# Half-precision parts in place of fp32r parts in the feed-forward of a fused attention and max-out kernel

## The chip, the cores and the metric

The kernel runs on one core of a Trainium2 chip. The metric is the device time of one execution in microseconds. The engines are named as the profile names them: PE (TensorE, matrix products; PEld is its weight loads), DVE (VectorE), ACT (ScalarE), POOL (GpSimd) and SP (SyncE, which here only issues DMAs).

## The reference

Two stages follow each other. The first is a linear attention with a decaying state, token by token, for 4 sequences, 8 heads, 768 tokens and 48 channels per head. The second takes its output as 3072 tokens of 384 features through three 384 x 768 products, an element-wise maximum, and a 768 x 384 product.

```python
for t in range(S):
    kt, vt, rt = (k[:, :, t], v[:, :, t], r[:, :, t])
    cur = np.einsum('bhd,bhe->bhde', u[None] * kt, vt)
    y[:, :, t] = np.einsum('bhd,bhde->bhe', rt, state + cur)
    state = w[None, :, :, None] * state + np.einsum('bhd,bhe->bhde', kt, vt)
...
h = np.maximum(np.maximum(x @ w1, x @ w2), x @ w3)
return (h @ w_out).astype(np.float32)
```

The inputs of the attention are float32; the four weight matrices are float64. k, r and v are normal with a spread of 0.1, the decay w lies between 0.85 and 0.95, and the weights have a spread of one over the square root of their row count.

## The kernel before, in words

**Work.** The 768 tokens of each sequence are cut into 12 chunks of 64, so that a chunk is 256 tokens of the 4 sequences. For each chunk there are two halves q (4 heads each). Per half the attention makes scores (L412, r against k within the chunk, masked), values (L449, scores against v plus r against the state) and keys (L432, k against v, added to the state at L438). All of this is done in pairs of half-precision parts: each float32 operand is a high part and a low part, and `three` (L408) adds high x high, high x low and low x high, 64 or 48 columns each. The left operands kb, ktb, vb and sb are block matrices that `spread` (L319) makes by two DMAs from the dense kd, ktd, vd and sd. In chunk 0 the products are plain float32 instead (`full`, L479).

**Feed-forward.** The values of both halves become the feature-major x of a chunk in two parts, xh (ACT, L464) and xl (DVE, L468), both fp32r. For each of 6 blocks f of the hidden size and each of the 3 matrices, `up` (L490) adds 9 products of 128 x 128 weights against 256 tokens: xh and xl against the high weights, xh against the low weights. ACT copies the first of three results out of PSUM (L499), DVE takes the maximum with the second and the third (L503). The hidden value m is split into hh (ACT, L506) and hl (POOL or DVE, L512), and `down` (L524) makes three output tiles of 18 products each. A chunk thus has 162 products up and 54 down, 216 of 256 columns, and the kernel 2592. An fp32r product is one instruction that loads its own weights.

**Weights.** The float64 weights come in 16 half tiles of 590 KB. For each, ACT and DVE in turn do `tops` (L240), `convert` (L243), `round_up` (L247, high part) and `leave` (L250, low part); all of this falls into chunks 0 and 1. They are loaded a second time near the end for a test of their lowest bits (L262, L266).

**Guards.** Sums of squares of r, k, v and the state (L348, on ACT) and some other numbers are compared with limits at the end (`check`, L554); a one-column product counts the partitions that pass (L565), DVE makes a flag (L569), and every engine reads it into a register (L911). If a partition fails, a general, slow part (L576) computes everything again.

**Order.** The order of all instructions is fixed before the kernel is built. Each step is given to `Plan.do` with an engine, a due time in chunks, a cost and the buffers it takes; `Plan.order` lays them out engine by engine, and the table `SHIFT` moves the due time of each kind of step. Every engine then works strictly through its own list. For chunks 0 to 2 the scaling of k and r, the product r u k and the decay (L367, L386, L387, L406) stand on DVE; from chunk 3 on they stand on POOL (L361).

Of the kernel before, what the change touches and what calls it, by code (L numbers as in the profile page):

```python
# [8 lines left out]
F32R = mybir.dt.float32r  # L9
# [25 lines left out]
SC_X = 2.0 ** -23  # L35


class Plan:
# [21 lines left out]
    }  # L60

    def __init__(self, bufs):
        self.bufs, self.todo, self.wrote, self.read = bufs, [], {}, {}

    def do(self, due, eng, cost, fn, reads=(), writes=(), takes=(), size=0, near=0):
# [6 lines left out]
        late = due > self.OPENING  # L72
        due += self.SHIFT.get(kind, (0, 0))[late]
# [8 lines left out]
        self.todo.append(dict(n=n, due=due, eng=eng, cost=cost, fn=fn, need=need, takes=takes, size=size, near=near, kind=kind, late=late, touch={*reads, *writes, *new}))  # L82
# [68 lines left out]
def kernel(ctx, tc, feat, tok, wu, ut, ws, wo, cst, out):  # L151
    nc = tc.nc
    const = ctx.enter_context(tc.tile_pool(name="const", bufs=1))
    raw = ctx.enter_context(tc.tile_pool(name="raw", bufs=3))
# [5 lines left out]
    hp = ctx.enter_context(tc.tile_pool(name="hp", bufs=1))  # L160
    wld = ctx.enter_context(tc.tile_pool(name="wld", bufs=4))
# [85 lines left out]
    def round_up(n, h, raw):  # L247
        nc.scalar.copy(out=part_of(n, h)[0], in_=mids(raw).bitcast(F32))
# [37 lines left out]
    tkf = hp.tile([P, NP, 2, C], F32, name="hl")  # L286
# [58 lines left out]
    stat = const.tile([P, 4, 2 * NCH], F32, name="stat")  # L345
    nc.vector.memset(stat[:, 3], 0.0)

    def square_sum(src, kind, c, q, scale=1.0):  # L348
        junk = tmp.tile([P, U, D], BF16, name="junk", bufs=1)
        nc.scalar.activation(out=junk, in_=src, func=AF.Square, scale=scale, accum_out=stat[:, kind, 2 * c + q:2 * c + q + 1])  # L350
# [117 lines left out]
    def x_low(c, q, xh, xl):  # L468
        ps = raws[c, q].pop("va")
        for (hi, src), (lo, _) in zip(x_parts(xh, q, ps), x_parts(xl, q, ps)):  # L470
            nc.vector.scalar_tensor_tensor(out=lo, in0=src, scalar=SC_X, in1=hi.bitcast(F32), op0=ALU.mult, op1=ALU.subtract)  # L471
# [18 lines left out]
    def up(x, f, i, n):  # L490
        ps = psm.tile([P, n], F32, name="psm")
        prods = [(wup[:, f, i, j, :], t[:, j, :]) for j in range(NJ) for t in x]
        prods += [(by_up(lows[f], i, j), x[0][:, j, :]) for j in range(NJ)]
        pairs3(ps, prods)
        return ps

    def first(ps, n):
        m = tmp.tile([P, n], F32, name="m", bufs=3)
        nc.scalar.copy(out=m, in_=ps)  # L499
# [11 lines left out]
    def h_low(c, h, f, m):  # L511
        lows_by(c, f).tensor_tensor(out=h[1][:, f, :], in0=m, in1=h[0][:, f, :].bitcast(F32), op=ALU.subtract)  # L512

    def up_all(x, h, f, n):
        for i in range(3):
            ps = up(x, f, i, n)
            if i == 0:
                m = first(ps, n)
            else:
                least(ps, m, m)  # L520
        h_high(h, f, m)
        h_low(0, h, f, m)

    def down(h, m, fs, banks, n):  # L524
# [4 lines left out]
        prods = [(t, hh[:, f, :]) for f in fs for t in (wdn[:, f, ms], by_down(lows[NF + f // 3], f, ms))]  # L529
        prods += [(wdn[:, f, ms], hl[:, f, :]) for f in fs]  # L530
        pairs3(banks[m], prods, 0 in fs, NF - 1 in fs)

    def leaving(ps, n):
        o = tmp.tile([P, n], F32, name="io", bufs=3)
        nc.scalar.copy(out=o, in_=ps)  # L535
# [40 lines left out]
    def general():  # L576
        def convert_any(n, h):
            hi, lo = part_of(n, h)
            rw = load_weight(n, h).bitcast(I32)[:, 0:2 * HN].rearrange("p (n two) -> p n two", two=2)
            t = raw.tile([P, HN], I32, name="tok")  # L580
            e = raw.tile([P, HN], I32, name="tok")
            m = hp.tile([P, HN], I32, name="hh")
# [13 lines left out]
            t = t.bitcast(F32)  # L596
            nc.scalar.copy(out=hi, in_=t)
# [378 lines left out]
```

## Time and profile before

| what | value |
|---|---|
| median of 3 runs (lowest to highest) | 414.68 us (414.3 to 416.64) |
| span of the profiled execution | 413.4 us |
| PE busy, of the span | 393.2 us, 95% |
| DVE busy | 283.6 us, 69% |
| ACT busy | 256.1 us, 62% |
| POOL busy | 183.2 us, 44% |
| DMA, mean | 218 GB/s, 90.08 MB |

The span runs from the first to the last instruction. It is 1.28 us under the median of the runs; that difference stands here for what lies around the span. Busy time of PE is that of matmuls whose ends overlap, so the rate of PE is read from the starts of successive matmuls in the timeline and not from the mean duration of one. The first feed-forward product starts at 28.97 us; what is ahead of it is loading, the float32 attention of chunk 0 and the first weights.

### The profile page before, as it was taken

To read this page: it belongs to the slowest core of one execution; us is meant where nothing else is said; L and a number is where in the kernel's file an instruction comes from. 1 tells how busy PE (TensorE), PEld (TensorE's weight loads), DVE (VectorE), ACT (ScalarE), POOL (GpSimd) and SP (SyncE) were. 2 spreads that over 40 slices of the span, in tenths; PEclk is the share of its full clock that TensorE was granted. 3 is DMA by queue.
4 is the path that set the end of the run, shared out by engine and by line. 5 is a ranking of instruction groups with operands and counts; after the bars stand their busy time and mean duration, and the time that the engine had idled before them with its cause. 6 is when DMAs were issued, how large, how long until landed. Compare 5 with 4: busy or idle time off the path is not lost.

```text
span 413.4 us, 11975 instructions
## 1 busy us (share of the span) xinstructions
PE 393.2 (95%) x4758; PEld 388.5 (94%) x4758; DVE 283.6 (69%) x550; ACT 256.1 (62%) x674; POOL 183.2 (44%) x180
## 2 busy tenths in 40 slices
PE   2869999999999999999999999999999999999996
PEld 2759999999999999999999999999999999999995
DVE  6888999988688766767667666567676596354240
ACT  5999987885766556456456456466456477265231
POOL 9000000298668754674664654754574551020120
PEclk9999999999999999999999999999999999999999
DMA  7899998889799997786785786785885996886101
GB/s 286 320 314 212 255 307 285 223 224 293 207 276 239 248 226 186 224 225 158 226 223 139 247 214 162 233 222 148 239 222 142 310 301 148 243 304 203 38 2 41
DMA packets 30954, 90.08 MB, mean 218 GB/s; under 512 B 4784, under 2 KB 9648, under 8 KB 30896
## 3 DMA queue, kind: packets, MB, share of 16 engines
q1 hardware_dynamic: 25568, 84.47, 72.1%
q10 hardware_dynamic: 5328, 4.82, 3.7%
q8 instruction: 38, 0.62, 0.7%
q14 instruction: 20, 0.16, 0.2%
HBM read 45.85 MB, written 4.72 MB: 122 GB/s over the span
## 4 chain that ended last, share of the span: by engine, by line
PE 65%; DVE 3%; ACT 3%; DMA 2%; issue 1%; POOL 1%; ACTq 0%; SPq 0%; DVEq 0%
PE psm L488 55%; PE psa L410 10%; DMA sb<-sd 2%; ACT junk L350 1%; DVE kd L338 1%; DVE state L446 0%; ACTq L874 0%; DVE m L503 0%; ACT io L535 0%; ACT xh L466 0%; DVE am L420 0%; POOL feat L367 0%; DVE hl L512 0%; ACT kd L333 0%; DVE sd L340 0%
## 5 line engine op out<-in xcount | busy, mean ns | idle before, releaser
L488 PE MATMUL psm<-xh,wh 128*128 128x256 f32 x648 | 166.6, 287 | 4.9 <-ACT xh L466 2.9
L488 PE MATMUL psm<-xl,wh 128*128 128x256 f32 x648 | 163.6, 282 | 1.1 <-DVE xl L471 1.1
L488 PEld LDWEIGHTS psm<-xh,wh 128*128 128x128 f32 x648 | 123.4, 190 | 5.7 <-ACT xh L466 3.1
L488 PEld LDWEIGHTS psm<-xl,wh 128*128 128x128 f32 x648 | 123.0, 190 | 1.4 <-DVE xl L471 1.4
L488 PE MATMUL psm<-xh,wl 128*128 128x256 f32 x648 | 112.9, 284 | 0.0
L503 DVE TENSOR_TENSOR m<-psm,m 128x256 f32<-128x256 f32 x144 | 60.4, 420 | 63.2 <-PE psm L488 54.5
L488 PEld LDWEIGHTS psm<-xh,wl 128*128 128x128 f32 x648 | 93.1, 190 | 0.0
L367 POOL TENSOR_TENSOR feat<-feat,wrt 128x512 f32<-128x512 f32 x36 | 47.1, 1319 | 74.7 <-DVE sd L340 68.9
L512 POOL TENSOR_TENSOR hl<-m,hh 128x256 fp32r<-128x256 f32 x55 | 46.5, 847 | 73.8 <-ACT hh L506 73.7
L506 ACT CAST hh<-m 128x256 fp32r<-128x256 f32 x72 | 28.8, 404 | 57.0 <-DVE m L503 56.7
L488 PE MATMUL psm<-hh,woh 128*128 128x256 f32 x216 | 54.3, 284 | 0.0
L488 PE MATMUL psm<-hh,wl 128*128 128x256 f32 x216 | 53.4, 279 | 0.0
L386 POOL TENSOR_TENSOR am<-tok,u_sb 128x384 f32<-128x384 f32 x18 | 21.0, 1165 | 58.0 <-DVE al L430 58.0
L350 ACT ACTIVATE junk<-tok 128x384 bf16<-128x384 f32 x72 | 37.5, 520 | 14.6 <-DMA tok<-in_tok_dram 12.0
L488 PEld LDWEIGHTS psm<-hh,woh 128*128 128x128 f32 x216 | 40.6, 188 | 0.0
L488 PEld LDWEIGHTS psm<-hh,wl 128*128 128x128 f32 x216 | 40.6, 188 | 0.0
L471 DVE SCALAR_TENSOR_TENSOR xl<-psa,xh 32x256 fp32r<-32x256 f32 (+2 forms) x60 | 28.3, 471 | 14.5 <-ACT xh L466 13.6
L466 ACT ACTIVATE xh<-psa 32x256 fp32r<-32x256 f32 (+2 forms) x60 | 25.0, 417 | 16.4 <-PE psa L410 15.4
L488 PE MATMUL psm<-hl,woh 128*128 128x256 f32 x216 | 35.1, 280 | 0.0
L338 DVE TENSOR_TENSOR kd<-feat,kd 128x512 f16<-128x512 f32 x22 | 20.5, 933 | 19.6 <-ACT kd L333 19.6
L410 PE MATMUL psa<-ah,vb 128*128 128x64 f16 x352 | 32.9, 194 | 0.0
L410 PE MATMUL psa<-rh,sb 128*128 128x64 f16 x352 | 32.5, 193 | 0.0
(98 smaller groups left out, 742.0 us busy)
## 6 DMA issues: line engine op xcount, KB each, us to landing
tok<-in_tok_dram SPq DMA_DIRECT2D x24, 576.0 KB, 6.8
raw<-in_ws_dram SPq DMA_DIRECT2D x24, 576.0 KB, 7.4
feat<-in_feat_dram SPq DMA_DIRECT2D x24, 512.0 KB, 5.4
kb<-kd SPq DMA_DIRECT2D x22, 256.0 KB, 5.9
kb<-kd SPq DMA_DIRECT2D x22, 248.0 KB, 6.1
ktb<-ktd SPq DMA_DIRECT2D x20, 256.0 KB, 3.4
ktb<-ktd SPq DMA_DIRECT2D x20, 248.0 KB, 4.5
raw<-in_wo_dram SPq DMA_DIRECT2D x8, 576.0 KB, 5.5
```

Of the source, the lines that this page charges most:

```text
L338: nc.vector.tensor_tensor(out=dense.dense[:, 1, :, 0:w], in0=src, in1=dense.dense[:, 0, :, 0:w], op=ALU.subtract)
L350: nc.scalar.activation(out=junk, in_=src, func=AF.Square, scale=scale, accum_out=stat[:, kind, 2 * c + q:2 * c + q + 1])
L367: helper(c).tensor_tensor(out=t[n], in0=t[n], in1=tb, op=ALU.mult)
L386: helper(c).tensor_tensor(out=w.rearrange("p (g b) d -> p g b d", g=2), in0=t["r"], in1=by_token(u_sb, q), op=ALU.mult)
L410: nc.tensor.matmul(out=ps, lhsT=l[i], rhs=rr[j], start=first and n == 0, stop=last and n == 2)
L466: nc.scalar.mul(out=hi, in_=src, mul=SC_X)
L471: nc.vector.scalar_tensor_tensor(out=lo, in0=src, scalar=SC_X, in1=hi.bitcast(F32), op0=ALU.mult, op1=ALU.subtract)
L488: nc.tensor.matmul(out=ps, lhsT=a, rhs=b, start=first and n == 0, stop=last and n == len(prods) - 1)
L503: nc.vector.tensor_tensor(out=to, in0=ps, in1=m, op=ALU.max)
L506: nc.scalar.copy(out=h[0][:, f, :], in_=m)
L512: lows_by(c, f).tensor_tensor(out=h[1][:, f, :], in0=m, in1=h[0][:, f, :].bitcast(F32), op=ALU.subtract)
```

## The change

Every operand of the feed-forward (x, h and all weights) becomes two half-precision parts instead of two fp32r parts. To fit half precision they are scaled by powers of two: x by 2^8, weights and h by 2^6. The scale factors are taken out again where PSUM is read anyway: the copy of L499 becomes a multiplication, the maximum of L503 a multiplication and a maximum in one instruction, the copy of L535 a multiplication. The numbers of products and columns stay; each half-precision product is now a weight load and a matmul, two instructions, as in the attention.

New guards: the squares of xh for each chunk (12 more square sums of 768 columns on ACT) and of each weight tile (8 of 1152 columns on ACT, in the last three chunks). The general part works in plain float32 and gets tiles of its own.

Weights and h now take half the room, and the room is given to buffers: `raw` (token tiles) 4 instead of 3, `raw64` (weights on arrival) 6 instead of 4, hh and hl 2 instead of 1 each.

The table that shifts due times has three stages instead of two, other numbers throughout, and a second table, `ONCE`, that moves single steps. The planned cost of a group of products is lower (1.075 to 0.993 for 9). The diff, without the general part and with a line or two of the tables:

```diff
-    OPENING = 1.6
+    STAGES = (1.6, 4)
     SHIFT = {
-        "act ah": (-5.31, -0.9), "act am": (2.08, 0), "act hh": (1.37, 0.4), "act his": (-0.69, 0), "act io": (-5.36, -2.55),
+        "act ah": (-52.95, 14.65, 8.9), "act am": (7.15, -25.65, 17.2), "act hh": (-9.55, -32.05, -3.85),
...
+    ONCE = {
+        "act am": {3: -5.5}, "act his": {2: -61.15}, "act ktb": {1: -45.5}, "act ktdh": {3: -20.5},
...
-    raw = ctx.enter_context(tc.tile_pool(name="raw", bufs=3))
+    raw = ctx.enter_context(tc.tile_pool(name="raw", bufs=4))
...
-    hp = ctx.enter_context(tc.tile_pool(name="hp", bufs=1))
-    wld = ctx.enter_context(tc.tile_pool(name="wld", bufs=4))
+    hp = ctx.enter_context(tc.tile_pool(name="hp", bufs=2))
+    wld = ctx.enter_context(tc.tile_pool(name="wld", bufs=6))
...
-    wup = const.tile([P, NF, 3, NJ, P], F32R, name="wh")
-    wdn = const.tile([P, NF, DM], F32R, name="woh")
...
-    lows = [const.tile([P, WN], F32R, name=f"wl{n}") for n in range(NW)]
+    wt = [const.tile([P, 2, WN], F16, name=f"w{n}") for n in range(NW)]
+    highs = [t[:, 0] for t in wt]
+    lows = [t[:, 1] for t in wt]
...
     def round_up(n, h, raw):
-        nc.scalar.copy(out=part_of(n, h)[0], in_=mids(raw).bitcast(F32))
+        nc.scalar.mul(out=part_of(n, h)[0], in_=mids(raw).bitcast(F32), mul=W16)
...
-        nc.vector.tensor_tensor(out=lo, in0=mids(raw).bitcast(F32), in1=hi.bitcast(F32), op=ALU.subtract)
+        nc.vector.scalar_tensor_tensor(out=lo, in0=mids(raw).bitcast(F32), scalar=W16, in1=hi, op0=ALU.mult, op1=ALU.subtract)
...
-        prods = [(wup[:, f, i, j, :], t[:, j, :]) for j in range(NJ) for t in x]
+        prods = [(by_up(highs[f], i, j), t[:, j, :]) for j in range(NJ) for t in x]
...
-        nc.scalar.copy(out=m, in_=ps)
+        nc.scalar.mul(out=m, in_=ps, mul=SC_M)
...
-    def least(ps, m, to):
-        nc.vector.tensor_tensor(out=to, in0=ps, in1=m, op=ALU.max)
+    def least(ps, m):
+        nc.vector.scalar_tensor_tensor(out=m, in0=ps, scalar=SC_M, in1=m, op0=ALU.mult, op1=ALU.max)
...
-                T["x", c] = [xp.tile([P, NJ, TOK], F32R, name="xh"), None]
+                T["x", c] = [xp.tile([P, NJ, TOK], F16, name="xh"), None]
...
+        if q:
+            do(due + 0.5, "act", act(NJ * TOK) + 0.1, lambda: square_sum(T["x", c][0].rearrange("p j n -> p (j n)"), XE + c, SC_E), reads=[hi], writes=[("sqx", c)])
...
-                    T["h", c] = [hp.tile([P, NF, TOK], F32R, name="hh")]
+                    T["h", c] = [hp.tile([P, NF, TOK], F16, name="hh")]
...
+    for n in range(NW):
+        do(NCH - 1.5 + 0.1 * n, "act", act(WN) + 0.1, lambda n=n: square_sum(highs[n], WE + n, 1.0 / W16), reads=[("begun", NCH - 2), *(("his", n, h) for h in range(2))], writes=[("sqw", n)])
```

The order of the instructions changes on every engine. Three places follow. The line numbers of after are higher by 24 to 28 up to `h_low` (L512, after L540) and by 14 to 22 behind it.

On PE at the start, before (feat, kb: float32 scores of a half; tok, ktb: its keys; am, vb: its values; psm: feed-forward):

```order
L296 MATMUL psa<-cs,hl 128x128 x4
L483 MATMUL psa<-feat,kb 128x64 x8
L483 MATMUL psa<-am,vb_141 96x64 x8
L483 MATMUL psa<-feat,kb 128x64 x8
L483 MATMUL psa<-tok,ktb 112x48 x8
L483 MATMUL psa<-am,vb_143 96x64 x8
L488 MATMUL psm<-xh,wh 128x256
```

The same place after:

```order
L320 MATMUL psa<-cs,tkf 128x128 x4
L511 MATMUL psa<-feat,kb 128x64 x8
L511 MATMUL psa<-tok,ktb 112x48 x8
L511 MATMUL psa<-am,vb_139 96x64 x8
L511 MATMUL psa<-feat,kb 128x64 x8
L511 MATMUL psa<-tok,ktb 112x48 x8
L511 MATMUL psa<-am,vb_141 96x64 x8
L516 LDWEIGHTS w_105
L516 MATMUL psm<-xh,w_105 128x256
```

The keys of the second half, which before came after the first nine feed-forward products, now stand ahead of the values of that half; the first 54 feed-forward products then follow without attention between them. Both f32 products and weight loads are shown as the program has them: an fp32r product has no LDWEIGHTS row of its own.

On ACT, what stands just ahead of xh of the second half of chunk 0, before (ztop, wh: weight steps; kd, vd, sd, rh: half-precision parts; junk: a square sum):

```order
L248 CAST wh<-raw_185 128x576
L248 CAST wh<-raw_187 128x576
L333 ACTIVATE kd<-feat 128x8x64
L444 ACTIVATE state<-psa 112x192 x2
L350 ACTIVATE junk,stat<-tok 128x384 x2
L350 ACTIVATE junk,stat<-state 128x384
L350 ACTIVATE junk,stat<-tok 128x384
L333 ACTIVATE sd<-state 128x8x48
L241 CAST ztop_114<-raw_270 128x576
L333 ACTIVATE vd_149<-tok 128x8x48
L466 ACTIVATE xh<-psa 96x256
L466 ACTIVATE xh<-psa 32x256 x3
```

and after:

```order
L265 CAST ztop_112<-raw_187 128x576
L272 ACTIVATE w_104<-raw_181 128x576
L272 ACTIVATE w_105<-raw_185 128x576
L272 ACTIVATE w_106<-raw_187 128x576
L265 CAST ztop_113<-raw_189 128x576
L472 ACTIVATE state<-psa 112x192 x2
L378 ACTIVATE junk,stat<-state 128x384
L272 ACTIVATE w_106<-raw_189 128x576
L357 ACTIVATE kd<-feat 128x8x64
L400 CAST rh<-feat 128x512
L494 ACTIVATE xh<-psa 96x256
L494 ACTIVATE xh<-psa 32x256 x3
```

Counted from the start of ACT's list to this xh, there are now 6 `tops` instead of 5, 6 `round_up` instead of 4, 4 copies into ktb instead of 2, 4 of the state instead of 2, one rh more, 8 square sums instead of 10, and one vd fewer. On DVE, ahead of xl of the same half, stand one `convert`, one `leave` and one rl more and one total, one decay and one vd fewer. Between x of chunk 0 and x of chunk 1 DVE has 54 instructions before and 55 after, and ACT 63 before and 60 after.

On ACT at the end, before:

```order
L911 TENSOR_LOAD flag
L506 CAST hh<-m 128x256
L499 COPY m<-psm 128x256
L506 CAST hh<-m 128x256
L535 COPY io<-psm 128x256
L874 DMA out_dram<-io 128x256
L535 COPY io<-psm 128x256
L874 DMA out_dram<-io 128x256
L535 COPY io<-psm 128x256
L874 DMA out_dram<-io 128x256
```

and after:

```order
L553 ACTIVATE io<-psm 128x256
L896 DMA out_dram<-io 128x256
L553 ACTIVATE io<-psm 128x256
L896 DMA out_dram<-io 128x256
L553 ACTIVATE io<-psm 128x256
L935 TENSOR_LOAD flag
L896 DMA out_dram<-io 128x256
```

The reading of the flag now stands between the last output tile and its DMA. On PE the one-column count (psa<-good,ones) is now the last product of all; before, 90 feed-forward products came after it.

More of the change, by code (lines that the diff above doesn't have):

```diff
@@ L34 @@
 SC_S = 2.0 ** -24
-SC_X = 2.0 ** -23
+SC_X = 2.0 ** -15
+X16 = 2.0 ** 8
+W16 = 2.0 ** 6
+H16 = 2.0 ** 6
+SC_M = H16 / (X16 * W16)
+SC_O = 1.0 / (H16 * W16)
+SC_E = 2.0 ** 2.5 / X16
 class Plan:
@@ L60 @@
     }
     def __init__(self, bufs):
-        self.bufs, self.todo, self.wrote, self.read = bufs, [], {}, {}
+        self.bufs, self.todo, self.wrote, self.read, self.count = bufs, [], {}, {}, {}
     def do(self, due, eng, cost, fn, reads=(), writes=(), takes=(), size=0, near=0):
@@ L71, in do @@
         kind = eng + " " + (made if isinstance(made, str) else made[0])
-        late = due > self.OPENING
-        due += self.SHIFT.get(kind, (0, 0))[late]
+        if kind in self.SHIFT:
+            due += self.SHIFT[kind][sum(due > t for t in self.STAGES)]
+        nth = self.count[kind] = self.count.get(kind, -1) + 1
+        due += self.ONCE.get(kind, {}).get(nth, 0)
         need = {self.wrote[k] for k in (*reads, *writes) if k in self.wrote}
@@ L81, in do @@
         need.discard(n)
-        self.todo.append(dict(n=n, due=due, eng=eng, cost=cost, fn=fn, need=need, takes=takes, size=size, near=near, kind=kind, late=late, touch={*reads, *writes, *new}))
+        self.todo.append(dict(n=n, due=due, eng=eng, cost=cost, fn=fn, need=need, takes=takes, size=size, near=near, kind=kind, touch={*reads, *writes, *new}))
     def order(self, free):
@@ L285 @@
     nc.vector.tensor_copy(out=wc, in_=pw[:, :, C])
-    tkf = hp.tile([P, NP, 2, C], F32, name="hl")
+    tkf = work.tile([P, NP, 2, C], F32, name="tkf")
     for hh in range(2):
@@ L343, with square_sum @@
     nc.gpsimd.memset(state, 0.0)
[L345 to L350, printed above, removed]
+    NS = 2 * NCH
+    RK, XE, WE, VE, SE = 0, 2 * NS, 2 * NS + NCH, 2 * NS + NCH + NW, 3 * NS + NCH + NW
+    ALL = SE + NS
+    stat = const.tile([P, ALL], F32, name="stat")
+    nc.vector.memset(stat[:, SE:ALL], 0.0)
+    def square_sum(src, at, scale=1.0):
+        junk = tmp.tile([P, WN], BF16, name="junk", bufs=1)
+        dst = junk[:, 0:U * D].rearrange("p (u d) -> p u d", u=U) if len(src.shape) == 3 else junk[:, 0:src.shape[1]]
+        nc.scalar.activation(out=dst, in_=src, func=AF.Square, scale=scale, accum_out=stat[:, at:at + 1])
     def units(a):
@@ L511, in h_low @@
     def h_low(c, h, f, m):
[L512 to L522, printed above, removed]
+        lows_by(c, f).tensor_tensor(out=h[1][:, f, :], in0=m, in1=h[0][:, f, :], op=ALU.subtract)
     def down(h, m, fs, banks, n):
@@ L534, in leaving @@
         o = tmp.tile([P, n], F32, name="io", bufs=3)
-        nc.scalar.copy(out=o, in_=ps)
+        nc.scalar.mul(out=o, in_=ps, mul=SC_O)
         return o
-    def xtile(n):
-        return [xp.tile([P, NJ, n], F32R, name=f"x{s}") for s in "hl"]
     def bounded(dst, src, lo, hi):
@@ L576, in general, with slowly @@
     def general():
+        with tc.tile_pool(name="gen", bufs=1) as gen:
+            slowly(gen)
+    def slowly(gen):
+        whole = [t.rearrange("p a n -> p (a n)").bitcast(F32) for t in wt]
         def convert_any(n, h):
-            hi, lo = part_of(n, h)
             rw = load_weight(n, h).bitcast(I32)[:, 0:2 * HN].rearrange("p (n two) -> p n two", two=2)
-            t = raw.tile([P, HN], I32, name="tok")
+            t = whole[n][:, h * HN:(h + 1) * HN].bitcast(I32)
             e = raw.tile([P, HN], I32, name="tok")
-            m = hp.tile([P, HN], I32, name="hh")
+            m = raw.tile([P, HN], I32, name="tok")
             ts = nc.vector.tensor_scalar
@@ L842, in mul @@
                     T["up", c, f, i] = up(T["x", c], f, i, TOK)
-                do(due + 0.035 * i, "pe", 1.075, mul, reads=[*x, *((a, f, h) for a in ("his", "lo") for h in parts[i])], takes=[("psm", ("up", c, f, i))])
+                do(due + 0.035 * i, "pe", 0.993, mul, reads=[*x, *((a, f, h) for a in ("his", "lo") for h in parts[i])], takes=[("psm", ("up", c, f, i))])
                 if i == 0:
@@ L870, in part @@
             bank = ("dn", c, m)
[L871 removed]
+            do(due, "pe", len(fs) * 0.331, lambda: down(T["h", c], m, fs, banks, TOK), reads=reads, **(dict(takes=[("psm", bank)]) if 0 in fs else dict(writes=[bank])))
             if NF - 1 in fs:
```

107 lines of the change are left out of this document (58 added, 49 removed), and 15 rows, old and new, of tables (ONCE, SHIFT).

## The prediction, made before the change was run

> **What bounds the kernel now.** I read the page first, then the chain that ended last, then a table by stretches.
>
> ```profile
> span 413.4 us, 11975 instructions
> ```
>
> ```profile
> 160.53 11.75 PE psm L488 x99
> 172.28 1.42 PE psa L410 x48
> 173.69 1.14 PE psm L488 x9
> 174.83 0.61 PE psa L410 x24
> 175.45 1.15 PE psm L488 x9
> 176.59 0.72 PE psa L410 x24
> 177.31 11.75 PE psm L488 x99
> 189.06 2.72 PE psa L410 x96
> ```
>
> From about 140 us the chain is PE alone: 216 feed-forward products (psm) and four blocks of attention (psa) per chunk. The stretches (length, then busy time and instructions of PE, PEld, DVE, ACT, POOL; clock, DMA share, GB/s) tell two stages apart; the DVE column is the one to look at.
>
> ```profile
> 5.80:31.50 25.70, 17.84 (x88) 16.48 (x86) 22.58 (x39) 23.80 (x54) 5.22 (x8) 1.00 0.91 332
> 31.50:61.60 30.10, 29.30 (x341) 28.82 (x341) 28.06 (x54) 27.65 (x69) 0.00 (x0) 1.00 0.96 261
> 61.60:100.70 39.10, 38.46 (x467) 38.02 (x467) 35.83 (x64) 30.70 (x85) 18.92 (x16) 1.00 0.88 256
> 100.70:140.00 39.30, 37.65 (x495) 36.92 (x494) 30.50 (x53) 25.78 (x71) 27.52 (x25) 1.00 0.89 235
> 140.00:376.00 236.00, 236.00 (x3070) 234.68 (x3069) 153.36 (x295) 134.58 (x363) 122.64 (x117) 1.00 0.79 218
> 376.00:398.00 22.00, 22.00 (x217) 22.00 (x214) 8.76 (x30) 9.28 (x24) 2.23 (x3) 1.00 0.19 70
> ```
>
> Until 100.7 us DVE is nearly as full as PE (28.06 of 30.10 us, then 35.83 of 39.10); behind 140 us PE never stops and DVE works 65% of the time. I therefore cost the change in stages, cut at the first product of chunk 2.
>
> **What a product costs.** From the timeline of PE, by starts:
>
> ```profile
> 200.16 0.28 PE L488 MATMUL psm<-xh,wh 128*128 128x256 f32 x1
> 202.28 0.28 PE L488 MATMUL psm<-xh,wh 128*128 128x256 f32 x1
> ...
> 203.35 0.20 PE L410 MATMUL psa<-ah,vb 128*128 128x64 f16 x1
> 203.39 0.19 PE L410 MATMUL psa<-al,vb 128*128 128x64 f16 x1
> ...
> 204.73 0.19 PE L410 MATMUL psa<-rh,sb 128*128 128x64 f16 x1
> 204.76 0.36 PE L488 MATMUL psm<-xh,wh 128*128 128x256 f32 x1
> 204.96 0.28 PE L488 MATMUL psm<-xl,wh 128*128 128x256 f32 x1
> ```
>
> ```profile
> 37.75 0.41 PE L488 MATMUL psm<-xh,wh 128*128 128x256 f32 x1
> 39.67 0.40 PE L488 MATMUL psm<-xh,wh 128*128 128x256 f32 x1
> ```
>
> Eighteen fp32r products lie between 200.16 and 202.28: 117.8 ns each. Nine lie between 37.75 and 39.67: 213.3 ns each; the array then ran at a lower clock. If that was half the clock, 256 columns take 106.7 ns at the full one, and fp32r pays 11.1 ns more. The half-precision products, 46 starts from 203.39 to 204.73, take 29.1 ns for 64 columns, of which a quarter of 106.7 is 26.7: they pay 2.4 ns, each with a weight load of its own. No row shows 256 half-precision columns. The bounds are 106.7 ns (nothing but the array) and 117.8 (the extra is no matter of type); I take 106.7 + 2.4 = 109.1, since the f16 rows of this trace carry exactly that loading scheme. The gain is 8.7 ns per product; the some 27 products ahead of 39.9 us, at 213 ns, gain nothing.
>
> A change of type costs too: the first f16 start after fp32r takes 0.040 instead of 0.029 us, and the second fp32r start after f16 comes after 0.20 instead of 0.118. That is 0.093 us per block, four blocks per chunk, 11 chunks: 4.1 us, which vanish.
>
> **Stage one, to the first product of chunk 2.**
>
> ```profile
> 28.97 0.58 PE L488 MATMUL psm<-xh,wh 128*128 128x256 f32 x1 [2.87 <-ACT xh L466]
> 30.65 0.58 PE L488 MATMUL psm<-xl,wh 128*128 128x256 f32 x1 [1.10 <-DVE xl L471]
> ...
> 32.67 3.23 PE L483 MATMUL psa<-tok,ktb 128*112 128x48 f32 x16
> 35.68 0.56 PE L488 MATMUL psm<-xh,wh 128*128 128x256 f32 x1
> ```
>
> ```profile
> 42.52 0.39 PE L488 MATMUL psm<-xh,wh 128*128 128x256 f32 x1 [0.80 <-ACT m L499]
> ```
>
> ```profile
> 61.90 0.28 PE L488 MATMUL psm<-xh,wh 128*128 128x256 f32 x1
> ```
>
> ```profile
> 100.66 0.28 PE L488 MATMUL psm<-xh,wh 128*128 128x256 f32 x1
> ```
>
> ```profile
> L350 ACT ACTIVATE junk<-tok 128x384 bf16<-128x384 f32 x72 | 37.5, 520 | 14.6 <-DMA tok<-in_tok_dram 12.0
> ```
>
> ```profile
> L241 ACT CAST ztop<-raw 128x576 f16<-128x576 bf16 x16 | 13.6, 847 | 0.1
> L372 ACT CAST rh<-feat 128x512 f16<-128x512 f32 x22 | 13.5, 614 | 0.2
> L248 ACT CAST wh<-raw 128x576 fp32r<-128x576 f32 x12 | 8.6, 718 | 1.6 <-DVE raw L245 1.6
> L477 ACT ACTIVATE ktb<-tok 64x384 f32<-64x384 f32 x4 | 2.1, 518 | 0.0
> ```
>
> PE waits for x of chunk 0, complete at 31.5 us. ACT now has more in front of its xh: one ztop (0.85), two round_up (1.44), two ktb copies (1.04), one rh (0.61), against two square sums (1.04); the small copies of the state and of v about cancel. That is 2.9 us; ACT was idle 1.9 of the 25.7 us, so the delay is 1.0 to 2.9. I take 2.2: x complete at 33.7. The keys of the second half, 3.0 us (32.67 to 35.68), are now done ahead of it, so the tenth product starts at 33.7 + 8 x 0.213 = 35.4 instead of 35.68: no change within what I can tell.
>
> The way to chunk 1 took PE 26.2 us (35.68 to 61.90). 133 products at the full clock give 1.2, four type changes 0.4, a stop (the row at 42.52) 0.8: PE could be at chunk 1 at 59.2. But x of chunk 1 comes after 55 DVE instructions where there were 54 (28.06 us): 33.7 + 28.1 = 61.8 if DVE never idles, 63.8 if it idles 2.0 as before. I take 62.8: PE stops for 3.6 us. From there chunk 2 was 38.8 us away; 270 products give 2.3, five changes 0.5, the idle time of PE in that stretch 0.6: 35.4, so 98.2. DVE, at 35.83 us busy with 64 instructions, would have x of chunk 2 at 62.8 + 35.8 = 98.6 without idling. I take 98.6: **stage one gains 2.1 us**, between 6 (nothing is late) and -1. The work on DVE and ACT hides behind nothing here: it is the bound that takes the gain away.
>
> A stop may cost more than its length. The Trainium skill, page "TensorE: Matmul & The Clock Gate", section "Part 1: The HAM clock gate (the 'warmup' mystery)", says that an idle window of about 3.4 us drops the array to half its clock until a window of work has passed. The 213 ns rows ahead of 39.9 us fit that; no stop behind them was that long here, so no run shows whether 3.6 us would do it.
>
> **Stage two, chunk 2 to the last product.** 2160 products x 8.7 ns = 18.8 us, and the other 35 type changes 3.3 us: **22.1 us**. Other engines have room: DVE 65%, ACT 57% of the steady stretch, 7% more in the shorter one. What is added hides there: per chunk a square sum of 768 columns (0.52 us for 384, so under 1.1), and 8 of 1152 columns (about 1.6 each, 13 us) in the last chunks, where ACT had 9.28 us of 22. The maximum as multiply-and-maximum may cost DVE up to 0.1 us more on each of 144; 14 us over 290 are hidden behind chunk 2, ahead of it 36 of them would be 3 us late. More buffers cost nothing.
>
> **The end.**
>
> ```profile
> L911 ACTq TENSOR_LOAD <-flag x1: 471/471/471, 399.0 to 399.0; - x1
> ```
>
> ```profile
> 409.40 0.37 ACT io L535
> ```
>
> ```profile
> 409.81 0.40 ACTq L874 DMA_DIRECT2D out_dram<-io  x1
> ```
>
> The last output DMA now waits behind the reading of the flag, which waits for the count, the last product of PE. From the last product to that issue took 0.45 us; count, flag and the 0.47 us of reading make some 0.95: **0.5 us lost**. Its bounds are 0.3 and 1.
>
> **The sum.** 413.4 - 2.1 - 22.1 + 0.5 = 389.7 us of span, and 1.28 us around it as before: 391.0 us.
>
> **The rivals.**
>
> *PE is never late* (0.22). DVE and ACT idle less in the new order and x of chunk 1 comes with 1 us of stop instead of 3.6; the short stops behind chunk 2 go as well (39.30 - 37.65 = 1.7 us, and what refilling PE takes, about 2 in all). Then 391.0 - 2.6 - 2 = 386.4. For it: more weight buffers and a second h buffer let steps move. Against: the 55 instructions remain.
>
> *The early bound holds on* (0.15). DVE idles as before (1.0), the maximum is dearer (3.0 by chunk 2), and the stop brings back the low clock for some 4 us, as it held from 35.68 to 39.9 (19 products x 0.104 = 2.0): 397.0. This is what the clock gate of the page above would add to.
>
> *Half precision gains nothing at 256 columns* (0.04). The extra 11 ns stays; only the type changes go: 413.4 - 4.1 + 2 (a later x) + 0.5 + 1.28 = 413.1, no change.
>
> *Weight loads come into the open* (0.03, slower). There are 2592 more instructions on PE, weight loads that fp32r did not list.
>
> ```profile
> L410 PEld LDWEIGHTS <-sb 128*128 128x128 f16 x528 | 27.5, 98 | 0.0
> ```
>
> If all 98 ns of each lay open, a product would take 107 + 98 = 205 ns and the kernel some 226 us more, 640 us; it turns slower than before from about 9 ns open each. Against it: pairs of load and product in the attention start every 29.1 ns, with 64 columns to hide the load, and here are 256.
>
> The Trainium skill, same page, section "LDWEIGHTS (loading the stationary operand)", gives columns over 1.2 as the nanoseconds of a load, 107 for these 128 columns, which speaks for this rival; by it alone every load would be as long as its product. The 29.1 ns pairs contradict that figure for f16 loads here.
>
> *The guards fail* and the general part runs (0.01, slower by milliseconds: 768 dependent token steps with DMAs). Against: 1152 weights of variance 1/384 give sums of 3.0, those of variance 1/768 give 1.5, well inside 0.35 to 15.
>
> **How the numbers follow.** My forecast has 0.55, 391.0 us. Its own bounds are those of stage one (6 to -1 instead of 2.1) and a ns either way on a product (2.6 us). The range has to reach to the first and second rival and leave the last three out: 385 to 398. A measurement here tells about 0.5%, 2.1 us, from no change. Faster: 0.55 + 0.22 + 0.15 = 0.92; same 0.04; slower 0.04.
>
> **What would show it.** Right: psm starts 109 ns apart in the steady stretch, 29 ns at every change between 64 and 256 columns, chunks 29.1 us apart instead of 31.2, a first product of chunk 1 that waits for DVE's xl near 62.8 us, chunk 2 at 98.6, and the last output DMA behind a TENSOR_LOAD. Wrong: starts of 107 or 118 ns, or stops of PE behind 100 us that before had not, above all for PSUM tiles that ACT has yet to empty while it does the weights' squares.

## The result and the profile after

The changed kernel takes 428.57 us (median of four runs, 427.69 to 434.02) beside 414.92 for the kernel before: a ratio of 1.034, with a 95% interval from 1.028 to 1.041. It is slower, where 391.0 us was forecast. The profiled execution took 427.69 us. Its page (span, busy time, granted clock in 40 slices, chain that ended last):

```profile
span 425.9 us, 12008 instructions
...
PE 377.8 (89%) x4758; PEld 335.8 (79%) x4758; DVE 284.7 (67%) x550; ACT 274.9 (65%) x714; POOL 178.2 (42%) x180
...
PEclk9999999999979999999999898899999999999999
...
PE 35%; DMA 27%; DVE 16%; ACT 10%; issue 6%; POOL 2%; SPq 2%; ACTq 1%; DVEq 0%; POOLq 0%
```

The chain of the kernel before, from its page:

```profile
PE 65%; DVE 3%; ACT 3%; DMA 2%; issue 1%; POOL 1%; ACTq 0%; SPq 0%; DVEq 0%
```

DVE is as busy as before in all, ACT 19 us more, and PE is busy 15 us less in a longer span. What is new is the second entry of the chain: transfers (DMA) take 27% of it, where they took 2% before and PE alone made the chain behind 140 us. The same stretches as in the prediction show the same thing by place:

```profile
31.50:61.60 30.10, 26.45 (x334) 21.54 (x334) 29.54 (x60) 27.14 (x70) 0.00 (x0) 1.00 0.91 261
61.60:100.70 39.10, 37.42 (x484) 33.88 (x483) 34.96 (x62) 30.20 (x85) 19.07 (x17) 1.00 0.89 253
100.70:140.00 39.30, 32.80 (x458) 29.06 (x456) 24.62 (x45) 22.30 (x63) 20.38 (x20) 0.91 0.81 205
140.00:376.00 236.00, 215.91 (x2977) 192.22 (x2975) 154.29 (x289) 141.43 (x376) 121.57 (x116) 0.97 0.76 217
```

From 100.7 us PE stops all along and the granted clock is below 1. In the long stretch DVE is as busy as before (154 of 236 us) and ACT 7 us more (141), so neither of the two is full.

The products themselves do what was forecast. From PE's timeline, by starts:

```profile
202.12 0.19 PE L438 MATMUL psa<-rh,sb 128*128 128x64 f16 x1
202.15 0.27 PE L516 MATMUL psm<-xh,w 128*128 128x256 f16 x1
202.26 0.27 PE L516 MATMUL psm<-xl,w 128*128 128x256 f16 x1
202.37 0.27 PE L516 MATMUL psm<-xh,w 128*128 128x256 f16 x1
```

They start 0.11 us apart (109 ns as the median of the trace's starts), and the step from 64 to 256 columns takes 0.03 us.

What does PE wait for? In the kernel before, from 100 to 410 us, these are all of its waits (in total, times, longest, in us):

```profile
PE psm L488 <- ACT io L535: 0.9, 2, 0.7
PE psa L410 <- DVE rl L377: 0.8, 1, 0.8
```

The longest waits of PE, then some of SP's DMA queue, in the whole changed kernel (the second of PE's belongs to the start and was 5.2 us before):

```profile
PE psa L438 <- DMA ktb<-ktd: 17.9, 8, 6.0
PE psa L320 <- DVE stat L373: 5.5, 1, 5.5
PE psa L438 <- DVE al L458: 3.8, 5, 1.6
```

```profile
SPq L204 <- DVE kd L362: 62.3, 13, 9.6
...
SPq L344 <- DVE ktd L362: 15.8, 6, 4.0
```

and SP's queue in the kernel before, L320 being the spreads and L176 the load of feat:

```profile
SPq L320 <- PE psa L410: 85.0, 18, 8.0
...
SPq L176 <- DVE rl L377: 9.1, 12, 4.6
```

Before, SP mostly stood at a spread that was ready and only waited for PE to have read the old tile: the spreads were early. Now it stands 62.3 us at the load of feat (L204), which waits until DVE has made `kdl` (L362) from the old tile in one of the two feat buffers. Thirteen times what stands behind that load in the queue, mostly spreads, waits with it. One such place, SP's queue by the timeline:

```profile
97.47 0.59 SPq L345 DMA_DIRECT2D kb<-kd  x1
107.74 0.33 SPq L204 DMA_DIRECT2D feat<-in_feat_dram  x1
108.11 0.46 SPq L344 DMA_DIRECT2D sb<-sd  x1
...
109.32 0.99 SPq L344 DMA_DIRECT2D ktb<-ktd  x1
```

with, on DVE and on PE,

```profile
103.02 0.55 DVE L364 SCALAR_TENSOR_TENSOR sd<-state,sd 128x384 f16<-128x384 f32 x1
...
103.83 0.54 DVE L362 TENSOR_TENSOR ktd<-tok,ktd 128x384 f16<-128x384 f32 x1
...
106.94 0.73 DVE L362 TENSOR_TENSOR kd<-feat,kd 128x512 f16<-128x512 f32 x1 [1.77 <-ACT kd L357]
```

```profile
111.34 0.19 PE L438 MATMUL psa<-rh,kb 128*128 128x64 f16 x1
117.54 1.12 PE L438 MATMUL psa<-vd,ktb 128*128 128x48 f16 x24 [6.01 <-DMA ktb<-ktd]
```

The parts of the state and of the keys were ready at 103.6 and 104.4 us. Their spreads left at 108.1 and 109.3, because the load ahead of them waited for `kd` at 107.7. PE needed ktb at 111.5 and got it at 117.5.

### The profile page after: what moved, and what is told of

The parts are those of the page before. It is cut to its first block, busy times and chain, and to the rows that moved or that the text cites. A ratio compares the mean times of both kernels' runs of the same rounds, so it can differ in the third digit from the quotient of the medians.

```text
span 425.9 us, 12008 instructions
## 1 busy us (share of the span) xinstructions
PE 377.8 (89%) x4758; PEld 335.8 (79%) x4758; DVE 284.7 (67%) x550; ACT 274.9 (65%) x714; POOL 178.2 (42%) x180
## 4 chain that ended last, share of the span: by engine, by line
PE 35%; DMA 27%; DVE 16%; ACT 10%; issue 6%; POOL 2%; SPq 2%; ACTq 1%; DVEq 0%; POOLq 0%
PE psm L516 29%; DMA ktb<-ktd 10%; DMA kb<-kd 8%; PE psa L438 5%; DMA tok<-in_tok_dram 4%; ACT junk L378 3%; DVE m L531 2%; DMA out_dram<-io 2%; DVE w L276 2%; DMA feat<-in_feat_dram 2%; DVE raw L269 1%; DVE kd L362 1%; DVE al L458 1%; ACT ztop L265 1%; DVE feat L395 1%
## 5 line engine op out<-in xcount | busy, mean ns | idle before, releaser
L516 PEld LDWEIGHTS <-w 128*128 128x128 f16 x2592 | 253.7, 99 | 44.4 <-issue 10.0
L516 PE MATMUL psm<-xh,w 128*128 128x256 f16 x1296 | 228.6, 277 | 3.9 <-ACT xh L494 1.7
L516 PE MATMUL psm<-xl,w 128*128 128x256 f16 x648 | 157.6, 278 | 2.3 <-DVE xl L499 2.2
L540 POOL TENSOR_TENSOR hl<-m,hh 128x256 f16<-128x256 f32 x55 | 41.0, 748 | 164.0 <-ACT hh L534 162.7
L531 DVE SCALAR_TENSOR_TENSOR m<-psm,m 128x256 f32<-128x256 f32 x144 | 60.3, 420 | 52.2 <-PE psm L516 38.3
L395 POOL TENSOR_TENSOR feat<-feat,wrt 128x512 f32<-128x512 f32 x36 | 50.5, 1413 | 35.7 <-DMA feat<-in_feat_dram 35.7
L516 PE MATMUL psm<-hh,w 128*128 128x256 f16 x432 | 56.7, 275 | 2.3 <-ACT hh L534 2.3
L378 ACT ACTIVATE junk<-tok 128x384 bf16<-128x384 f32 x72 | 37.4, 520 | 26.4 <-DMA tok<-in_tok_dram 25.5
L438 PE MATMUL psa<-al,vb 128*128 128x64 f16 x176 | 31.2, 193 | 3.8 <-DVE al L458 3.8
L516 PE MATMUL psm<-hl,w 128*128 128x256 f16 x216 | 34.0, 277 | 0.2
L438 PEld LDWEIGHTS <-vb 128*128 128x128 f16 x528 | 29.2, 98 | 5.2 <-issue 4.7
L499 DVE SCALAR_TENSOR_TENSOR xl<-psa,xh 32x256 f16<-32x256 f32 (+2 forms) x60 | 28.3, 471 | 5.2 <-ACT xh L494 4.4
L438 PE MATMUL psa<-rl,sb 128*128 128x64 f16 x176 | 31.2, 193 | 0.0
```

Source lines behind the costliest of these rows:

```text
L378: nc.scalar.activation(out=dst, in_=src, func=AF.Square, scale=scale, accum_out=stat[:, at:at + 1])
L395: helper(c).tensor_tensor(out=t[n], in0=t[n], in1=tb, op=ALU.mult)
L438: nc.tensor.matmul(out=ps, lhsT=l[i], rhs=rr[j], start=first and n == 0, stop=last and n == 2)
L516: nc.tensor.matmul(out=ps, lhsT=a, rhs=b, start=first and n == 0, stop=last and n == len(prods) - 1)
L531: nc.vector.scalar_tensor_tensor(out=m, in0=ps, scalar=SC_M, in1=m, op0=ALU.mult, op1=ALU.max)
```

## The experiments

The theories that the runs were to tell apart: **A**, the new order costs the time and half precision itself gains what was forecast; as **A1**, PE's attention blocks stand too close behind their spreads, or as **A2**, the spreads are issued late. **B**, half precision itself costs it: shorter products reach the spreads sooner in any order, and the guards and the dearer maximum fill ACT and DVE.

**e1: the old tables.** The planner lays the steps out anew with the costs and buffers of the changed kernel, so this is not the order of the kernel before step by step.

```diff
-    STAGES = (1.6, 4)
+    STAGES = (1.6,)
     SHIFT = {
-        "act ah": (-52.95, 14.65, 8.9), "act am": (7.15, -25.65, 17.2), "act hh": (-9.55, -32.05, -3.85),
+        "act ah": (-5.31, -0.9), "act am": (2.08, 0), "act hh": (1.37, 0.4), "act his": (-0.69, 0), "act io": (-5.36, -2.55),
...
+    ONCE = {}
```

> The changed kernel with the two-column table of shifts of the kernel before (and its one border at 1.6), without the table of single instructions; half precision, guards and buffers stay. Theory A (the new order costs the time, half precision itself gains some 22 us behind chunk 2): 388 to 393 us, and stops of PE behind 41 us of under 8 us in all. Theory B (shorter products reach the spread DMAs sooner whatever the order, and the added guards and the multiply-and-maximum fill ACT and DVE): 414 us or more, with stops of PE for ktb as in the changed kernel.

409.73 us, ratio to the kernel before 0.986 (0.982 to 0.990). Between the two theories: from the first product of chunk 2 to the last product it took 288.9 us (115.54 to 404.45) where the kernel before took 308.7, a gain of 19.8; but chunk 2 began at 115.5, 15 us late. The steady order from the old tables is good for half precision, their opening with the new buffers is not.

**e2: no table of single steps.** `ONCE = {}`, all else as changed.

> The changed kernel without the table of single instructions (ONCE empty), the three-column shifts stay. If the corrections of single instructions make the stops (they were found for one particular course of events): 390 to 400 us. If the three-column shifts do: 420 to 435 us, with PE waiting for ktb in chunks 3 to 9 as in the changed kernel. Theory B: no change, 425 to 431.

423.09 us, ratio 1.019 (1.015 to 1.023); stops for kb and ktb remain (the longest is 4.8 us for ktb, up to 201.2 us). The three-stage shifts carry most of the loss.

**e3: the old order on PE alone.**

```diff
-        "pe ke": (-69.3, -5.8, -29.3), "pe sc": (-40.1, -23.6, -26.95), "pe turned": (6.05, 47.25, -45.6),
+        "pe ke": (-1.11, 0.1, 0.1),
...
```

> The changed kernel in which only TensorE's steps take the shifts of the kernel before (the late column for both later stages) and lose their single corrections; every other engine and the DMA queue keep the new tables. Theory A1 (TensorE's attention blocks stand too close behind their spread DMAs): 390 to 400 us, PE waiting for ktb under 4 us in all where the changed kernel waits 17.9. Theory A2 (the spread DMAs are issued late, behind loads on SP and behind late work of ACT and DVE): above 412 us, the waits for ktb stay. Theory B: 425 or more.

Two runs, 411.19 and 417.76 us, 1.6% apart: too far for a time to be taken from them. In the trace, which is of the longer one, PE's wait for ktb fell to 1.1 us behind 40 us, but it waited for ACT's `ah` (5.7) and for x (6.1) instead. That doesn't tell A1 from A2.

**e4 and e7: more buffers for the loads, every order unchanged.**

```diff
-    raw = ctx.enter_context(tc.tile_pool(name="raw", bufs=4))
+    raw = ctx.enter_context(tc.tile_pool(name="raw", bufs=5))
...
-        f = raw.tile([P, 2, 2, B, C], F32, name="feat", bufs=2)
+        f = raw.tile([P, 2, 2, B, C], F32, name="feat", bufs=3)
```

(e7 has the second pair only. Both: two scratch tiles of the general part with one buffer instead of two.)

> The changed kernel, every engine's order as it was, with three buffers for feat instead of two and five for tok instead of four, so that a load at the head of SP's queue finds a free buffer and lets the spreads behind it go (two scratch tiles of the general part, which doesn't run, share one buffer each, to make room). Theory A2 in its narrow form (spreads stand behind a load that waits for its buffer): 400 to 410 us, the SP queue's wait at the feat load falls from 62.3 to under 15 us and PE's wait for ktb from 17.9 to under 6. Theory A1 and theory B: within 4 us of the changed kernel, 424 to 432.

> The changed kernel, every engine's order as it was, with three buffers for feat only (tok stays at four). If the wait at the head of SP's queue is the one for feat (62.3 us at the feat load): 399 to 405 us, most of what e4_more_load_buffers gave. If the fifth tok buffer did it: 420 us or more.

e4: 400.47 us, ratio 0.965 (0.960 to 0.969). e7: 400.79 us, ratio 0.964 (0.960 to 0.968). The third feat buffer alone, one 4 KB tile per partition, takes 28 us from the changed kernel. SP's queue in e7, at the same place as above:

```profile
96.37 0.60 SPq L345 DMA_DIRECT2D kb<-kd  x1
97.07 0.75 SPq L204 DMA_DIRECT2D feat<-in_feat_dram  x1
102.96 0.46 SPq L344 DMA_DIRECT2D sb<-sd  x1
...
104.55 0.46 SPq L344 DMA_DIRECT2D ktb<-ktd  x1
```

The load goes at once, and each spread goes when DVE has made its parts, ktb 4.8 us earlier. SP waits at the load of feat for 3.0 us in all, and never for `kd`. The waits of PE in e7:

```profile
PE psa L438 <- DMA kb<-kd: 3.9, 3, 2.4
...
PE psa L438 <- DMA ktb<-ktd: 2.2, 4, 0.9
```

The transfers of ktb themselves became quicker too, though not as quick as in the kernel before (3.4 and 4.5 us). The DMA issues on the page of the changed kernel, then of e7 (KB each, median us from issue to landing):

```profile
ktb<-ktd SPq DMA_DIRECT2D x20, 256.0 KB, 6.7
ktb<-ktd SPq DMA_DIRECT2D x20, 248.0 KB, 7.1
```

```profile
ktb<-ktd SPq DMA_DIRECT2D x20, 256.0 KB, 5.8
ktb<-ktd SPq DMA_DIRECT2D x20, 248.0 KB, 6.1
```

No instruction moved on any engine or on SP's queue, no work was taken away, and the kernel turned from slower than before to faster. This shows A2 in its narrow form: a load that waits for its buffer at the head of SP's queue is the cause. What the runs do not separate is how much of the 28 us comes by the spreads behind the load and how much by the load's own data, which come earlier too: POOL's wait for feat fell from 35.7 to 11.7 us, and ACT's for tok, which is loaded behind feat, from 25.5 to 4.8. On the chain of the changed kernel behind 100 us, spreads make 82.5 us and the loads of feat and tok 23.5.

**e5: the new opening with the old steady order.** Up to a due time of 2.6 the new columns; behind it the old late column plus 60.

```diff
-    STAGES = (1.6, 4)
+    STAGES = (1.6, 2.6)
...
-        "act ah": (-52.95, 14.65, 8.9),
+        "act ah": (-52.95, 14.65, 59.1),
...
```

> The changed kernel with the new tables up to a due time of 2.6 and, behind it, the late column of the kernel before plus 60 for every kind (the 60 keeps later steps behind earlier ones). The new opening had the first product of chunk 2 at 98.1 us; the old steady order took 288.9 us from there to the last product in e1_old_order; with 4.8 us behind it and 1.3 around it that is 393 us, 390 to 396. Rival (the opening that the new tables make leaves transfers and buffers behind that a regular order can't use, so stops go on): 405 us or more.

409.82 us, ratio 0.987 (0.984 to 0.990): the rival's number, but the stops do not go on as it had it. From chunk 5 to chunk 10 a chunk took 29.2 to 29.9 us; chunk 2 took 40.1, with a wait of 5.3 us for ktb behind 111.4 us. There SP stood at the load of feat until 107.78, for the same `kd` of DVE.

**e6: the old tables with the old buffers too.** The planner counts raw64, hh and hl as in the kernel before, but still four token tiles, where this kernel has three.

```diff
-    raw = ctx.enter_context(tc.tile_pool(name="raw", bufs=4))
+    raw = ctx.enter_context(tc.tile_pool(name="raw", bufs=3))
...
-    hp = ctx.enter_context(tc.tile_pool(name="hp", bufs=2))
-    wld = ctx.enter_context(tc.tile_pool(name="wld", bufs=6))
+    hp = ctx.enter_context(tc.tile_pool(name="hp", bufs=1))
+    wld = ctx.enter_context(tc.tile_pool(name="wld", bufs=4))
```

> e1_old_order with the buffer counts of the kernel before too (three tok, four raw64, one of hh and hl each). If the larger buffers let the planner pull weight work ahead of x and so spoil the old opening (chunk 2 at 115.5 us in e1_old_order): chunk 2 at 98 to 102 us and 393 to 399 us in all. If the opening is late for the added work of half precision on ACT and DVE: chunk 2 above 110 us and 405 us or more.

405.94 us, ratio 0.976 (0.971 to 0.982). Chunk 2 began at 100.04 us, as in the kernel before: the larger buffers had spoiled the opening in e1, since the planner orders by them. But chunk 2 took 42.7 us: there too the loads stood at the head of SP's queue (feat until 108.4, tok until 114.2), and PE waited twice for kb. So half precision with the old tables meets the block as well, in one place. Whether shorter products alone bring it, as B says, is not shown: the planner's new costs changed the order of SP's queue too, and the wait for tok can come from the fourth token tile that the planner counted.

**e8: the changed kernel without its new guards.**

```diff
-            do(due + 0.5, "act", act(NJ * TOK) + 0.1, lambda: square_sum(T["x", c][0].rearrange("p j n -> p (j n)"), XE + c, SC_E), reads=[hi], writes=[("sqx", c)])
+            do(due + 0.5, "act", act(NJ * TOK) + 0.1, lambda: None, reads=[hi], writes=[("sqx", c)])
```

> The changed kernel without the square sums of x and of the weights (19 instructions of ACT left out, their places in the statistics set to 1, so x and weights are not guarded), all else as it was. If the guards cost nothing, as the prediction had it: within 2.5 us of the changed kernel, 426 to 431. If they hold ACT's steps and through them the spreads: 418 us or less.

431.39 us, ratio 1.038 (1.031 to 1.044), no faster than with them: here the guards cost nothing, and that half of B falls.

**e9 to e12: the block removed from other orders.** e9 is e5 with the third feat buffer, e10 has the fifth tok buffer as well, e11 is the kernel before with a third feat buffer, e12 is e6 with a third feat and a fourth tok buffer; the edits are those of e4.

> e5_new_opening_old_steady with a third feat buffer, order unchanged. Theory A2 (a load at the head of SP's queue waits for its buffer, and the spreads wait behind it): the stops at 111.4 us (5.5 us, ktb) and 166.0 (3.3, kb) of that run go, and with them its two stretches at half clock; 405 us of span become 391 to 396, and the run 393 to 398 us. Rival (these stops come from the spreads' own lateness, DVE's and ACT's steps ahead of them): 403 us or more.

> The same with a fifth tok buffer too. A2: equal to e9_mixed_feat3 or up to 3 us faster, since the wait at the feat load was by far the longer one. If earlier loads crowd the spreads on the DMA engines: slower than e9_mixed_feat3 by 2 us or more.

> The kernel before with a third feat buffer, nothing else. Its SP queue waited 85.0 us at spreads for a PSUM-side buffer that TensorE had yet to free and 9.1 at the feat load, so the spreads were early. A2: no change within 0.5% (413 to 417 us): the block needs the faster products or the new order. If a third buffer helps any order: 410 or less.

> e6_old_order_old_buffers (half precision in the kernel before's order) with a third feat and a fourth tok buffer. There the loads at 108.4 and 114.2 us waited for DVE's kd and ktd, kb came late twice, and chunk 3 took 42.7 us from chunk 2 where the kernel before took 34.6. A2: that stretch falls to 31 to 35 us and the run to 394 to 398 us. Rival (DVE's steps themselves are late there): it stays above 38 us, and the run above 402.

e9: 401.27 us, ratio 0.969 (0.964 to 0.974). e10: 399.98 us, 0.963 (0.960 to 0.966), the lowest median, though e4, e7, e9 and e16 lie within the noise of it. e11: 415.21 us, 0.999 (0.997 to 1.002), no change, as A2 had it. e12: 401.0 us, 0.965 (0.962 to 0.969). In e9 the stop behind 111.4 us went and a wait of 3.7 us for kb, up to 163.2, stayed; 393 to 398 was missed by 3. In e12 the stretch of chunk 2 fell from 42.7 to 35.4 us, and the run stayed 3 us above the range. e12 and e11 use the same tables and differ by half precision with its guards, by one tok buffer and by the order that the planner makes of its new costs: 14.2 us in all. In e10 chunks 6 to 8 are as regular as in the kernel before. The first products of chunks 7, 8 and 9, by PE's timeline:

```profile
254.57 0.27 PE L558 MATMUL psm<-xh,w 128*128 128x256 f16 x1
...
283.55 0.27 PE L558 MATMUL psm<-xh,w 128*128 128x256 f16 x1
...
312.53 0.27 PE L558 MATMUL psm<-xh,w 128*128 128x256 f16 x1
```

They lie 28.98 us apart.

**e13, e15, e16: what is left.** Five kernels with the block removed (e4, e7, e9, e10, e12), in three different orders, ended at 400 to 401 us, 9 to 10 above the forecast. Two theories for the rest: R1, spreads land late behind loads on the same DMA engines; R2, DVE's and ACT's steps are late. e13 and e15 change what the planner counts with, e16 takes the guards out of e10.

```diff
-    RATE, BEFORE, BEHIND = 275e3, 1.5, 0.9
+    RATE, BEFORE, BEHIND = 275e3, 1.5, 1.9
```

> e10_mixed_feat3_tok5 with one number of the planner changed: a transfer counts as landed 1.9 us behind its last byte, not 0.9, so TensorE's attention blocks move back where a spread is late in the plan. Theory R1 (what is left of the loss are spreads that land later than planned, behind loads on the same 16 DMA engines): PE's wait for kb falls from 6.7 us to under 2 and the run from 400.0 to 394 to 397 us. Theory R2 (what is left are DVE's and ACT's steps): 399 to 402 us.

> The same idea, stronger: the planner is told 240 KB/us instead of 275 and 1.9 us, and the old steady order begins at a due time of 2.0; the opening changes with it. R1: 392 to 398 us if the opening stays as it was (chunk 2 near 98 us). R2, or an opening that falls apart with other costs: 399 us or more.

> e10_mixed_feat3_tok5 without the square sums of x and of the weights (19 instructions of ACT; their places in the statistics set to 1, so x and weights are not guarded). In the changed kernel they cost nothing, but there SP's queue held everything up. If they cost nothing here either: 399 to 401 us. If ACT's 1 us per chunk ahead of the spreads is part of what is left (R2): 397 us or less.

e13: 403.89 us, ratio 0.971 (0.969 to 0.973). PE's wait for kb went, as R1 said, and the time did not come down: it waited for xl (5.7 us) and al (4.1) of DVE instead. That is above the range of R2 as well. e15: 416.84 us, 1.002 (1.001 to 1.004): chunk 1 began at 82.9 us, the opening fell apart, so it tells nothing about R1. e16: 399.99 us, 0.962 (0.960 to 0.963), equal to e10, though the work it leaves out is 23 us of ACT (20 square sums, not the 19 of the expectation, each with a short read of its total). In e10, by line and form:

```profile
L420 ACT ACTIVATE junk<-xh 128x768 bf16<-128x768 f16 x12 | 10.0, 837 | 0.2
L420 ACT ACTIVATE junk<-w 128x1152 bf16<-128x1152 f16 x8 | 9.3, 1158 | 0.1
```

R1 falls in its simple form, and R2 as far as the guards go.

## Why the prediction was wrong, point by point

| | first product of chunk 2 | from there to the last product | behind it | span |
|---|---|---|---|---|
| before | 100.66 | 308.7 | 4.0 | 413.4 |
| forecast | 98.6 | 286.6 | 4.5 | 389.7 |
| after | 98.07 | 323.0 | 4.8 | 425.9 |
| e7, one more feat buffer | 98.74 | 296.6 | 4.5 | 399.8 |
| e10, also the old steady order | 99.86 | 294.6 | 4.7 | 399.1 |

The last product is a feed-forward one before and the one-column count in the changed kernel, e7 and e10.

**The price of a product and of a type change: right.** 109 ns and no extra at a change, as the rows of 202 us show; a steady chunk of 28.98 us in e10 is 31.23 less 216 x 8.7 ns and 4 x 0.093 us.

**Stage one: right for DVE, wrong for what PE does meanwhile.** Chunk 2 began at 98.07, forecast 98.6, and DVE was full up to chunk 1 (29.54 of 30.10 us). The rows of the start:

```profile
30.43 0.37 PE L516 MATMUL psm<-xh,w 128*128 128x256 f16 x1 [1.67 <-ACT xh L494]
32.81 0.37 PE L516 MATMUL psm<-xl,w 128*128 128x256 f16 x1 [2.01 <-DVE xl L499]
```

```profile
31.92 1.75 DVE L499 SCALAR_TENSOR_TENSOR xl<-psa,xh 96x256 f16<-96x256 f32 x4
```

DVE had x of chunk 0 complete at 33.67 (forecast 33.7), of chunk 1 at 61.87 (62.8) and of chunk 2 at 98.39 (98.6). But PE does not wait for the whole of x: it takes the parts as they come. The tenth product started at 34.52 instead of 35.4, and chunk 1 at 60.57, ahead of its last part of x. The single stop of 3.6 us did not come; between 36 and 61 us PE had several gaps of at most 1.1 us between starts, none of them a wait for x of more than 0.5. From there to chunk 2 PE took 37.5 us instead of 35.8, so the sum came out within 0.6 us in part by luck.

**Stage two: this is the step that failed.** "Other engines have room: DVE 65%, ACT 57% of the steady stretch … What is added hides there." As far as it goes the sentence holds: leaving out the guards gains nothing (e8, e16), and the maximum takes 420 ns as before:

```profile
L531 DVE SCALAR_TENSOR_TENSOR m<-psm,m 128x256 f32<-128x256 f32 x144 | 60.3, 420 | 52.2 <-PE psm L516 38.3
```

What it leaves out is the order. The step costed what was added to each engine and nothing of what was moved on SP's queue, where the load of feat had come to stand ahead of spreads at points at which its buffer isn't free. A share of busy time shows no such place. That term was set at 0 and cost 28 us, what e7 gains by a buffer alone, of the 37.6 us between forecast and result. Part of it is the clock: in the changed kernel four stretches ran at half of it, and what their products took beyond 109 and 29 ns (some 213, and 40 to 54) comes to 7.7 us; e7 has one such stretch left, 1.4 us.

"More buffers cost nothing" can fail as well, in another way: in e1 they let the planner fill the opening of the old tables with other work, and chunk 2 began 15 us later than in e6, which has the old counts. For the changed kernel itself no run shows such a cost.

**The end: right within its bounds.** io is copied at 421.00 and its DMA issued at 421.85, 0.89 us behind the end of the last feed-forward product (420.96), where 0.95 was forecast. From that product to the end of the span it is 4.94 us where it was 4.05: 0.9 us lost, forecast 0.5 with bounds of 0.3 and 1.

```profile
421.00 0.38 ACT L553 ACTIVATE io<-psm 128x256 f32<-128x256 f32 x1 [1.05 <-PE psm L516]
...
421.85 0.34 ACTq L896 DMA_DIRECT2D out_dram<-io  x1
```

**The rivals.** None of them was what happened. The slower one had weight loads in the open, which the 109 ns rule out (both traces list 4758 weight loads, so the loads that the program adds were there before too). A load that holds up a queue was the mechanism to look for; the prediction named stops behind 100 us only as a sign of being wrong, and looked for them at PSUM tiles.

**What stays open.** With the block gone, e10's span is 9.4 us above the forecast: 1.3 by chunk 2, 6.1 in chunks 2 to 5, 2.0 in chunk 9, nothing in chunks 6 to 8. In chunks 2 to 5 e13 traded waits for kb for waits for xl and al, and no order tried here was free of both kinds. So the cause of these 9 us is not shown. Whether the new order would block with the longer fp32r products was not tried.

## What to carry to other kernels

A queue that works in order is a resource like an engine: for every load in it, ask which buffer it needs, which instruction frees that buffer, and what stands behind the load meanwhile. When the bound engine gets faster, list how early each of its transfers was (here: a queue that waits for PE is early, one that waits for DVE is not), since that lead is what the gain is paid from. Where two buffers make a load wait, a third one costs a line and some room (4 KB per partition here), changes no order, and tells at once whether the wait was the cause.

## What was not expected of the hardware

The clock falls after shorter stops than expected, and by place. Two stops of the changed kernel, then one of e10, cut into stretches of 3.41 or 6.83 us (length, busy time of PE, PEld, DVE, ACT, POOL; the number behind them is the granted clock):

```profile
111.90:115.31 3.41, 0.00 (x0) 0.00 (x0) 0.40 (x1) 0.00 (x0) 1.49 (x2) 1.00 1.04 232
115.31:122.14 6.83, 4.60 (x42) 3.58 (x43) 3.77 (x7) 2.76 (x7) 3.72 (x5) 0.50 1.02 241
231.36:234.77 3.41, 1.36 (x12) 0.91 (x10) 1.22 (x3) 2.43 (x7) 0.83 (x1) 1.00 0.96 225
234.78:238.19 3.41, 3.41 (x24) 2.49 (x23) 1.46 (x3) 1.78 (x5) 0.00 (x0) 0.50 0.44 120
```

```profile
159.29:162.70 3.41, 1.93 (x53) 1.76 (x51) 1.22 (x2) 1.64 (x5) 3.33 (x4) 1.00 1.02 266
162.71:166.12 3.41, 1.69 (x31) 1.40 (x32) 1.68 (x4) 3.29 (x10) 3.41 (x4) 1.00 1.02 313
166.12:169.53 3.41, 3.41 (x40) 3.07 (x38) 3.02 (x6) 2.54 (x9) 0.57 (x2) 1.00 0.54 113
```

A gap of 2.2 us between two starts (231.26 to 233.50) brought 3.41 us at half clock, one of 3.3 us (161.03 to 164.36, e10) none. The clock changed at multiples of 3.41 us from its first change, in every run here. Over all 17 traces it fell 34 times behind that first change (the fall at the end of each trace left aside), each time at the end of such a window in which PE was idle for 59% or more (an estimate from its starts, with 109 ns for a product of 256 columns and 29 for a smaller one, and about twice that at half clock). Where it stayed, PE was idle for at most 58% of the window, but for one window of 61%. The stop in e10 lay across two windows and left each of them idle for between five and six tenths. So in these runs it matters where a stop lies in the grid, and some six tenths of one window are enough.

The Trainium skill, page "TensorE: Matmul & The Clock Gate", section "Part 1: The HAM clock gate (the 'warmup' mystery)", speaks of one idle window of about 3.4 us. The length of the window agrees with the 3.41 us here; if it is read as a window that is idle as a whole, that does not agree.
